# Ordering TensorE's pieces by width inside a visit, and charging changes of kind in the plan of a fused attention and MLP kernel

## The chip, the cores and the metric

The kernel runs on one core of one Trainium2 chip. The metric is the device time of one execution, in microseconds (us). The kernel before takes 345.28 us, the median of three runs (344.76 to 346.15).

## The reference, cut to what matters

Eight batches of eight heads attend over 576 tokens of width 64, with 16 extra "beacon" keys and values in front that every query may see; the token keys are causal. The result goes, token by token with its heads side by side, through an MLP of 512, 2048 and 512 columns with a sigmoid gate.

```python
k_all = np.concatenate([beacon_k, k], axis=2)           # 592 keys
v_all = np.concatenate([beacon_v, v], axis=2)
scores = 1/np.sqrt(D) * np.matmul(q, k_all.transpose(0, 1, 3, 2))
scores = np.where(causal, -1000000000.0, scores)        # beacons are never masked
a = np.exp(scores - scores.max(-1, keepdims=True))
a /= a.sum(-1, keepdims=True) + 1e-09
x = np.matmul(a, v_all).transpose(0, 2, 1, 3).reshape(B * S, H * D)   # 4608 x 512
h = x @ w_in                                            # 4608 x 2048
out = (h * (1.0 / (1.0 + np.exp(-1.702 * h)))) @ w_out  # 4608 x 512
```

## The kernel before, in words

**Sets.** Four heads of one batch make a *set*; there are 16 sets, two to a batch. For each set GpSimd's queue (POOL) loads q and k, with each head on 32 partitions and the two halves of the width as neighbouring elements. VectorE (DVE) transposes both (a *turn*, line 343). Beacon keys come by other queues, are cast (line 328) and transposed too (line 336). TensorE (PE) then makes scores with keys on the partitions and queries along the columns, four heads side by side in the array: a *quad* of four matmuls, one per head, 32 rows each, twice (`d` = 0 and 1, line 362). ScalarE (ACT) takes the exp into `E` (line 374). Masks set what is not causal to zero: on DVE for sets 0 and 1 (line 388), on POOL for all others (line 395). The maximum is not subtracted.

**Pieces and chunks.** A set has five key blocks of 128. Causality leaves, for queries 0 to 287, pieces of 288, 176 and 48 columns, and for queries 288 to 575 pieces of 288, 288, 288, 208 and 80: 1664 columns, one after the other in `E`. Scores are made in *chunks* of up to 512 columns into a PSUM tile `s` that exists once, so the next chunk waits for the exp of the one before. Sets 0 to 3 have four chunks each (512, 384, 384, 384). From set 4 on chunks of 512 run on from set to set, so one chunk may hold the end of one set and the start of the next, in pieces as they fall. There are 55 chunks, and `qk`*i* is chunk *i*.

**Sums and values.** `av`*s.x.half* (line 447) multiplies `E` of set *s* with values: *x* = 0 and 1 are the two halves of the width, *x* = 2 is a product with ones that gives the row sums; the output of one head is 32 columns wide. From set 4 on DVE first adds the key blocks of `E` together (`zadd`, line 426) into `zs`, so that *x* = 2 needs one or two quads instead of three to five: pieces of 112 (from `E`) and 176 (from `zs`) for the first half, 288 for the second. DVE turns sums into factors (`z1`: a transpose, line 458; `z2`: reciprocal, line 463, and a transpose, line 467) and multiplies them into `xT` while leaving PSUM (`norm`, line 476).

**MLP.** Groups of tokens, two of 256 and then eight of 512, go through `m1`*.g.n* (line 498, `xT` times `w_in`, 4 matmuls of 512 columns or 8 of 256), a tanh on ACT (line 512), a `gate` on DVE (line 519), and `m2`*.g.mt.qt* (line 531), a scale on ACT (line 545) and a store from SyncE's queue (SP, line 551).

**PSUM.** Beside `s` there is a ring of four buffers `u`. Every `m1`, every `av` and every `m2` row of 128 tokens takes one, and it is free again when its last reader is done: `gate`, `z1` or `norm`, or the scale of the output.

**What sets the order.** `Plan` is a list scheduler that runs while the program is built (lines 21 to 151). Each operation has an engine, an estimated duration, dependences, a priority `pr` (lower goes first) and a due time before which it isn't taken. The plan runs all engines in modelled time and the instructions are then emitted in that order, so each engine executes its own list in order. On PE, `choose` (line 129) prefers scores and values over the MLP, and stays with one *kind*: `r` for scores (32 rows), `c` for sums and values (32 columns), `m` for the MLP (the full array). A row of operations of one kind is a *visit*. A change of kind is charged 110 ns if the MLP is on one side and 90 otherwise:

```python
if o.mode != mode:
    dur += 110 if "m" in (mode, o.mode) else 90
```

On the other engines the ready operation of the lowest `pr` is taken (line 102). Chunks from the ninth on are due at equal steps from `T_ATT0` = 13000 to `T_ATT1` = 255000 ns of the plan's time (line 554), and loads, turns and casts have due times before that. Loads are all issued on POOL, at most eight in flight (line 565), between the masks of that engine.

Of the kernel before, what the change touches and what calls it, by code (L numbers as in the profile page):

```python
# [10 lines left out]
ALU = mybir.AluOpType  # L11


class Op:
    __slots__ = (
        "eng", "dur", "deps", "pr", "due", "emit", "kind", "ring", "mode", "lat",
        "start", "end", "left", "users", "ready", "seq", "name",
    )


class Plan:
# [8 lines left out]
        self.tiles = {}  # L30
        self.closers = {}

    def op(self, eng, dur, deps, emit, kind="", pr=5, due=0, ring=None, closes=None, mode=None, name=""):
        o = Op()
        o.eng, o.dur, o.emit, o.kind, o.pr, o.due = eng, dur, emit, kind, pr, due
        o.ring, o.mode, o.name = ring, mode, name
# [23 lines left out]
    def run(self):  # L60
# [3 lines left out]
        for o in self.ops:  # L64
            if o.left == 0:
                avail[o.eng].append(o)
        mode, last = "m", ""
        order = []
        todo = len(self.ops)
        while todo:  # L70
# [28 lines left out]
            if e == "PE":  # L99
                o = self.choose(ok, t, mode, last, free)  # L100
            else:
                o = min(ok, key=lambda o: (o.pr, o.ready, o.seq))
            dur = o.dur
            if e == "PE":
                if o.mode != mode:
                    dur += 110 if "m" in (mode, o.mode) else 90
                mode, last = o.mode, o.kind
                if o.ring is not None and o.ring not in self.tiles:
                    self.tiles[o.ring] = slot[1]
                    self.bank[slot[1]] = o.ring  # L110
# [44 lines left out]
def kernel(  # L155
# [11 lines left out]
    nc = tc.nc  # L167
# [90 lines left out]
    for s in range(EARLY, NSET):  # L258
# [75 lines left out]
    def e_turn(s, which):  # L334
# [10 lines left out]
            in_=f32(src[:, :]).rearrange("p (t c) -> p t c", t=TR),  # L345
        )

    def e_qk(i):
        sc = pss.tile([P, Q, 512], F32, tag="s", name="s")
        ss[i] = sc  # L350
        o = 0
        for (s, c0, c1) in CHUNKS[i]:
            if s not in Es:
                Es[s] = ep.tile([P, Q, ETOT], F16, tag="E", name="E")
            for (j, a, e), col in zip(PIECES, ecol):
                u, v = max(c0, col), min(c1, col + e - a)
                if u >= v:
                    continue
                for d in range(2):
                    for h in range(Q):  # L360
                        r = 32 * h
                        nc.tensor.matmul(  # L362
                            sc[:, h, o : o + v - u],
                            kT[s % NB2][r : r + 32, j * P : (j + 1) * P, d],
                            qT[s % NB2][r : r + 32, a + u - col : a + v - col, d],
                            start=(d == 0),
                            stop=(d == 1),
                        )
                o += v - u

    def e_exp(i, n):
        s, c0, c1 = CHUNKS[i][n]
# [55 lines left out]
    def e_av(s, x, half):  # L428
        b, hs = divmod(s, HS)
        u = ring_tile(("av", s, x, half))  # L430
        E = Es[s]
        q0 = half * HF
        terms = []
        if x == 2 and s >= ZSUM:
            if half == 0:
                terms.append((P, 0, Z0, E, 0, True, True))
                terms.append((P, Z0, HF, zsum[s], 0, True, True))
            else:
                terms.append((P, 0, HF, zsum[s], ZW, True, True))
        else:  # L440
            n = len(AVP[half])
            for i, (j, a, e) in enumerate(AVP[half]):
                terms.append((min(P, NK - j * P), a - q0, e - q0, E, where(j, a), i == 0, i == n - 1, j))
        for kw, a, e, src, col, first, last, *j in terms:
            for h in range(Q):
                lhs = ones[0:kw, :] if x == 2 else vb[b % NB2][0:kw, j[0], Q * hs + h, x::2]
                nc.tensor.matmul(  # L447
                    u[32 * h : 32 * h + 32, a:e],
                    lhs,
                    src[0:kw, h, col : col + e - a],  # L450
                    start=first,
                    stop=last,
                )
# [171 lines left out]
    def chunk(i):  # L625
# [8 lines left out]
        w = 0  # L634
        for s, c0, c1 in CHUNKS[i]:
            for (_, a, e), col in zip(PIECES, ecol):
                x = min(c1, col + e - a) - max(c0, col)
                w += max(45, 2 * x / 2.4 + 6) if x > 0 else 0
        qks[i] = op(
            "PE", w, deps, lambda: e_qk(i), kind="qk", pr=0,  # L640
            due=T_ATT0 + T_CH * (i - NCH0) if i >= NCH0 else 0, mode="r", name=f"qk{i}",
        )
        for n, (s, c0, c1) in enumerate(CHUNKS[i]):
            x = exps[(i, n)] = op(
# [17 lines left out]
    def values(s):  # L662
        b, hs = divmod(s, HS)
        whole = s >= ZSUM
        order = [(2, 0), (2, 1), (0, 0), (1, 0), (0, 1), (1, 1)] if whole else [
            (x, h) for h in range(2) for x in (2, 0, 1)
        ]
        sums, z2 = [], {}
# [17 lines left out]
        for n, (x, half) in enumerate(order):  # L686
# [10 lines left out]
            avs[(s, x, half)] = op(  # L697
                "PE", sum(y / 2.4 + 6 for y in w), deps,
                lambda x=x, half=half: e_av(s, x, half), kind="av",
                pr=(16 * s + (n if whole else 8 * half)) if s >= HS else half,  # L700
                ring=key, mode="c", name=f"av{s}.{x}.{half}",
            )
            if x == 2:
                z1 = op("DVE", 410, [avs[(s, x, half)]], lambda h=half: e_z1(s, h), pr=0, closes=key, name="z1")
# [129 lines left out]
```

## The time and the profile before

| | us |
|---|---|
| median of three runs | 345.28 |
| the profiled execution | 344.9 |
| its span, first to last instruction | 343.2 |
| TensorE busy | 324.3 |
| VectorE busy | 236.8 |
| ScalarE busy | 202.3 |
| GpSimd busy | 113.5 |
| matmuls, number | 3864 |
| TensorE clock granted | 0.998 |

The profiled execution is one run, and the profile's durations add up to its span; what lies around the span is the start and the end of the execution. In lines with a line number, "x" is the count of instructions, "out<-in" names what is written and read, and shapes are partitions x elements. PE's busy time is modelled at each matmul's end, so two matmuls that follow each other closely overlap in it; start to start is the measure of what they cost. DVE's and ACT's durations overlap the next one's by about 0.1 us too. An engine whose line says "idle before <-releaser" waited that long for the releaser named. "PEld" is the loading of weights into the array.

### The profile page before, as it was taken

Reading aid. Unit: us, or ns where it says so; the run is one execution under the profiler, and the core shown is the slowest. Engines: PE = TensorE matmul, PEld = TensorE weight load, DVE = VectorE, ACT = ScalarE, POOL = GpSimd, SP = SyncE. Lnnn points to the kernel's source line nnn. Section 1 sums busy time; section 2 is a strip of 40 time slices with the busy share of each in tenths; the row PEclk is TensorE's granted clock in tenths of the full one; section 3 lists DMA queues with packets and bytes.
Section 4 is the critical chain, followed back from the end, with each engine's and each line's share of the span. In section 5 each row is a group of like instructions: output and inputs, shape, how many; then the busy total and the mean of one; then the engine's idle time right before and its main releaser. Section 6 shows DMA issues by size and latency. Waiting matters only on the chain.

```text
span 343.2 us, 9086 instructions
## 1 busy us (share of the span) xinstructions
PE 324.3 (94%) x3864; PEld 166.6 (49%) x3864; DVE 236.8 (69%) x460; ACT 202.3 (59%) x245; POOL 113.5 (33%) x184
## 2 busy tenths in 40 slices
PE   0699899999899999999999999999999999999995
PEld 0476565545354545454554454445544454444442
DVE  3859778499958889889988788797854344453310
ACT  1585686786647774867776766765664224454421
POOL 8753593463415631812463227312110000000000
PEclk9999999999999999999999999999999999999999
DMA  7999999539042924970459509300000100000111
GB/s 128 165 204 209 190 198 124 107 46 122 3 103 64 155 39 107 66 139 3 72 61 145 99 33 128 77 33 32 32 32 32 61 32 31 33 31 31 55 59 71
DMA packets 54120, 28.76 MB, mean 84 GB/s; under 512 B 41280, under 2 KB 45376, under 8 KB 54080
## 3 DMA queue, kind: packets, MB, share of 16 engines
q0 software_dynamic: 47552, 18.49, 45.8%
q1 hardware_dynamic: 6464, 9.69, 7.9%
q8 instruction: 30, 0.49, 0.6%
q14 instruction: 10, 0.08, 0.1%
q10 hardware_dynamic: 64, 0.01, 0.0%
HBM read 37.22 MB, written 9.44 MB: 136 GB/s over the span
## 4 chain that ended last, share of the span: by engine, by line
PE 86%; DVE 5%; ACT 4%; DMA 2%; issue 1%; POOL 1%; SPq 1%; DVEq 0%; ACTq 0%
PE u L531 35%; PE u L498 34%; PE u L447 9%; PE s L362 8%; ACT E L374 3%; DMA bkf<-in_beacon_k_dram 2%; DVE g L519 1%; DVE qT L343 1%; DVE zs L426 1%; ACT sig L512 1%; DVE kT L343 1%; POOL E L395 1%; DVE zt L458 1%; SPq L322 1%; DVE rz L467 0%
## 5 line engine op out<-in xcount | busy, mean ns | idle before, releaser
L498 PE MATMUL u<-xT,w 128*128 128x512 f16 (+1 forms) x640 | 145.5, 360 | 1.6 <-DVE xT L476 0.9
L531 PE MATMUL u<-w,g 128*128 128x512 f16 x576 | 142.0, 379 | 0.4 <-DVE zt L458 0.4
L519 DVE SCALAR_TENSOR_TENSOR g<-sig,u 128x512 f16<-128x512 f16 x144 | 96.9, 681 | 59.9 <-ACT sig L512 59.4
L512 ACT ACTIVATE sig<-u 128x512 f16<-128x512 f32 x144 | 85.5, 598 | 82.8 <-PE u L498 77.9
L374 ACT ACTIVATE E<-s 128x2048 f16<-128x2048 f32 (+3 forms) x64 | 98.6, 1556 | 29.5 <-PE s L362 29.2
L498 PEld LDWEIGHTS <-w 128*128 128x128 f16 x640 | 60.7, 98 | 63.1 <-issue 3.1
L395 POOL TENSOR_SCALAR_AFFINE_SELECT E<-E 128x448 f16<-128x448 f16 (+2 forms) x84 | 48.8, 606 | 123.3 <-ACT E L374 116.6
L531 PEld LDWEIGHTS <-g 128*128 128x128 f16 x576 | 54.5, 98 | 65.1 <-issue 2.0
L362 PE MATMUL s<-qT,kT 32*128 32x288 f16 (+12 forms) x1352 | 35.8, 236 | 11.6 <-DVE qT L343 10.8
L362 PEld LDWEIGHTS <-kT 32*128 32x128 f16 x1352 | 24.4, 95 | 33.2 <-issue 21.4
L545 ACT ACTIVATE osb<-u 128x512 f32<-128x512 f32 x36 | 21.5, 597 | 23.7 <-PE u L531 23.7
L426 DVE TENSOR_TENSOR zs<-zs,E 128x192 f16<-128x192 f16 (+3 forms) x48 | 28.1, 585 | 5.5 <-ACT E L374 2.5
L476 DVE TENSOR_TENSOR xT<-u,rz 128x288 f16<-128x288 f32 x64 | 26.3, 448 | 7.9 <-PE u L447 7.3
L447 PE MATMUL u<-E,vb 128*32 128x288 f16 (+4 forms) x1024 | 29.2, 258 | 0.2 <-DVE g L519 0.2
L303 POOL DMA_DIRECT2D vb<-in_v_dram x32 | 27.2, 864 | 3.3 <-DMA qn<-in_q_dram 1.8
L447 PEld LDWEIGHTS <-vb 128*32 128x32 f16 (+1 forms) x1024 | 22.1, 98 | 5.4 <-issue 2.1
L343 DVE STREAM_TRANSPOSE kT<-kn 128x576 f32<-128x576 f32 x16 | 20.1, 1257 | 2.1 <-DMA kn<-in_k_dram 1.6
L426 DVE TENSOR_TENSOR zs<-E 128x704 f16<-128x704 f16 (+1 forms) x24 | 16.5, 688 | 5.4 <-POOL E L395 3.1
L343 DVE STREAM_TRANSPOSE qT<-qn 128x576 f32<-128x576 f32 x16 | 19.9, 1241 | 0.1
L467 DVE STREAM_TRANSPOSE rz<-rc 128x288 f32<-128x288 f32 x32 | 15.3, 478 | 1.1
L458 DVE STREAM_TRANSPOSE zt<-u 128x288 f32<-128x288 f32 x32 | 13.8, 458 | 2.3 <-PE u L447 2.1
L287 POOL DMA_DIRECT2D qn<-in_q_dram x16 | 9.0, 563 | 4.1 <-DMA vb<-in_beacon_v_dram 1.9
(27 smaller groups left out, 67.2 us busy)
## 6 DMA issues: line engine op xcount, KB each, us to landing
out_dram<-osb SPq DMA_DIRECT2D x36, 256.0 KB, 2.0
kn<-in_k_dram POOLq DMA_DIRECT2D x16, 288.0 KB, 6.5
qn<-in_q_dram POOLq DMA_DIRECT2D x16, 288.0 KB, 6.0
vb<-in_v_dram POOLq DMA_DIRECT2D x24, 128.0 KB, 5.1
w<-in_moe_w_in_dram POOLq DMA_DIRECT2D x8, 256.0 KB, 9.0
w<-in_moe_w_out_dram POOLq DMA_DIRECT2D x4, 512.0 KB, 13.7
vb<-in_v_dram POOLq DMA_DIRECT2D x8, 112.0 KB, 3.9
vb<-in_v_dram POOLq DMA_DIRECT2D x8, 80.0 KB, 5.1
```

The source lines that it names most:

```text
L303: nc.gpsimd.dma_start(out=t[0 : hi - lo, j, h0:h1, :], in_=v[b, h0:h1, lo:hi, :].rearrange("h n d -> n h d"),)
L343: nc.vector.transpose(out=f32(dst.rearrange("p n e -> p (n e)")).rearrange("p (r t) -> p t r", t=TR), in_=f32(src[:, :]).rearrange("p (t c ...
L362: nc.tensor.matmul(sc[:, h, o : o + v - u], kT[s % NB2][r : r + 32, j * P : (j + 1) * P, d], qT[s % NB2][r : r + 32, a + u - col : a + v - ...
L374: nc.scalar.activation(out=Es[s][:, :, c0:c1], in_=ss[i][:, :, o : o + c1 - c0], func=AFT.Exp, scale=0.125,)
L395: nc.gpsimd.affine_select(out=blk, in_=blk, compare_op=ALU.is_ge, fill=0.0, base=off + (Nb if j == 0 else 0), pattern=[[0, Q], [1, w]], ch ...
L426: nc.vector.tensor_tensor(out=t[:, :, o : o + w], in0=x, in1=y, op=ALU.add)
L447: nc.tensor.matmul(u[32 * h : 32 * h + 32, a:e], lhs, src[0:kw, h, col : col + e - a], start=first, stop=last,)
L476: nc.vector.tensor_tensor(out=xT[:, 2 * hs + x, t0 : t0 + HF], in0=rings[("av", s, x, half)][:, 0:HF], in1=zs[(s, half)][1][:, :], op=ALU. ...
L498: nc.tensor.matmul(u[:, o : o + w], w1t[:, kp, nt * P : (nt + 1) * P], xT[:, kp, t0:t1], start=(kp == 0), stop=(kp == NKT - 1),)
L512: nc.scalar.activation(out=sig[:, 0:w], in_=rings[("m1", g, n0)][:, 0:w], func=AFT.Tanh, scale=0.851)
L519: nc.vector.scalar_tensor_tensor(out=gts[g][:, n0:n1, 0:w], in0=sigs[(g, n0)][:, 0 : n * w].rearrange("p (n w) -> p n w", n=n), scalar=1.0 ...
L531: nc.tensor.matmul(o[:, :], gts[g][:, nt, mt * P : (mt + 1) * P], w2t[:, nt, :], start=(nt == 0), stop=(nt == NNT - 1),)
```

## The change

Seven edits, in two places of the kernel: what is issued, and how the plan orders it.

1. *Scores* (`qk_pieces`, new). The pieces of a chunk are sorted by falling width, over the sets in it; if the narrowest is over 64 columns wide, it is cut into one of 32 columns less and one of 32, which comes last.
2. *Sums from set 4 on.* The first half's product goes as 176 (from `zs`), 80 and 32 columns instead of 112 and 176, and the second half's is put ahead of the first's.
3. *Charge.* Each PE operation has a `tail`, the width of its last piece (0 for the MLP). A change of kind is charged 95 ns and 0.75 of the time that the last piece takes at 2.4 columns a ns.
4. *DVE's choice.* If the operation that would be taken has `pr` over 0, and one with `pr` 0 (`z1`, `z2`, masks, first turns) gets ready within 140 ns, that one is taken and DVE waits for it. `norm` of sets 0 and 1 gets `pr` 0.
5. *Chunks.* The first chunk of sets 0 and 1 counts as two parts (288 and 224 columns), so it has two exp instructions.
6. *Masks.* Of sets 0 and 1, DVE keeps the three masks of the first half; the three of the second half go to POOL.
7. *Due times.* Chunks are due from 11000 to 245000.

The program has 4104 matmuls instead of 3864, DVE 6 instructions less, ACT 2 and POOL 6 more; the orders of all engines but SP change.

```diff
+NEAR = 140
@@ Plan.run
             else:
                 o = min(ok, key=lambda o: (o.pr, o.ready, o.seq))
+                if e == "DVE" and o.pr > 0:
+                    near = [x for x in avail[e] if x.pr == 0 and max(x.ready, x.due) <= t + NEAR]
+                    if near:
+                        o = min(near, key=lambda o: (o.ready, o.seq))
+                        t = max(t, o.ready, o.due)
             dur = o.dur
             if e == "PE":
                 if o.mode != mode:
-                    dur += 110 if "m" in (mode, o.mode) else 90
-                mode, last = o.mode, o.kind
+                    dur += 95 + 0.75 * tail / 2.4
+                mode, last, tail = o.mode, o.kind, o.tail
@@ chunks
+    DVM = (0, 1, 2)
     EARLY, ZSUM = 2 * HS, 2 * HS
+    SPLIT = True
...
-        CHUNKS += [[(s, 0, EHALF)]] + [[(s, EHALF + cut * i, EHALF + cut * (i + 1))] for i in range(3)]
+        CHUNKS += [[(s, 0, HF), (s, HF, EHALF)] if SPLIT and s < HS else [(s, 0, EHALF)]] + [[(s, EHALF + cut * i, EHALF + cut * (i + 1))] for i in range(3)]
@@ scores
+    def qk_pieces(i):
+        got, o = [], 0
+        for (s, c0, c1) in CHUNKS[i]:
+            for (j, a, e), col in zip(PIECES, ecol):
+                u, v = max(c0, col), min(c1, col + e - a)
+                if u < v:
+                    got.append((v - u, s, j, a + u - col, o))
+                    o += v - u
+        got.sort(key=lambda x: -x[0])
+        w, s, j, a, o = got[-1]
+        if w > 64:
+            got[-1:] = [(w - 32, s, j, a, o), (32, s, j, a + w - 32, o + w - 32)]
+        return got
...
-            for (j, a, e), col in zip(PIECES, ecol):
...
+        for (w, s, j, a, o) in qk_pieces(i):
+            for d in range(2):
+                for h in range(Q):
...
@@ e_av
             if half == 0:
-                terms.append((P, 0, Z0, E, 0, True, True))
                 terms.append((P, Z0, HF, zsum[s], 0, True, True))
+                terms.append((P, 32, Z0, E, 32, True, True))
+                terms.append((P, 0, 32, E, 0, True, True))
@@ due times, masks, values
-    T_ATT0, T_ATT1 = 13000, 255000
+    T_ATT0, T_ATT1 = 11000, 245000
...
-                    eng = "DVE" if s < HS else "POOL"
+                    eng = "DVE" if s < HS and m in DVM else "POOL"
...
-        order = [(2, 0), (2, 1), (0, 0), (1, 0), (0, 1), (1, 1)] if whole else [
+        order = [(2, 1), (2, 0), (0, 0), (1, 0), (0, 1), (1, 1)] if whole else [
...
-                w = [HF] if half else [Z0, ZW]
+                w = [HF] if half else [ZW, Z0 - 32, 32]
...
-                    pr=1, closes=key, name="norm",
+                    pr=1 if s >= HS else 0, closes=key, name="norm",
```

More of the change, by code (lines that the diff above doesn't have):

```diff
@@ L16 @@
         "eng", "dur", "deps", "pr", "due", "emit", "kind", "ring", "mode", "lat",
-        "start", "end", "left", "users", "ready", "seq", "name",
+        "start", "end", "left", "users", "ready", "seq", "name", "tail",
     )
@@ L31, in __init__, with op @@
         self.closers = {}
-    def op(self, eng, dur, deps, emit, kind="", pr=5, due=0, ring=None, closes=None, mode=None, name=""):
+    def op(self, eng, dur, deps, emit, kind="", pr=5, due=0, ring=None, closes=None, mode=None, name="", tail=0):
         o = Op()
         o.eng, o.dur, o.emit, o.kind, o.pr, o.due = eng, dur, emit, kind, pr, due
-        o.ring, o.mode, o.name = ring, mode, name
+        o.ring, o.mode, o.name, o.tail = ring, mode, name, tail
         o.deps = [d for d in deps if d is not None]
@@ L66, in run @@
                 avail[o.eng].append(o)
-        mode, last = "m", ""
+        mode, last, tail = "m", "", 0
         order = []
@@ L350, in e_qk @@
         ss[i] = sc
-        o = 0
         for (s, c0, c1) in CHUNKS[i]:
@@ L354, in e_qk @@
                 Es[s] = ep.tile([P, Q, ETOT], F16, tag="E", name="E")
-            for (j, a, e), col in zip(PIECES, ecol):
[L356 to L369, printed above, removed]
+        for (w, s, j, a, o) in qk_pieces(i):
+            for d in range(2):
+                for h in range(Q):
+                    r = 32 * h
+                    nc.tensor.matmul(
+                        sc[:, h, o : o + w],
+                        kT[s % NB2][r : r + 32, j * P : (j + 1) * P, d],
+                        qT[s % NB2][r : r + 32, a : a + w, d],
+                        start=(d == 0),
+                        stop=(d == 1),
+                    )
     def e_exp(i, n):
@@ L633, in chunk @@
             deps += [exps[(i - 1, n)] for n in range(len(CHUNKS[i - 1]))]
[L634 to L638, printed above, removed]
+        ps = [x[0] for x in qk_pieces(i)]
+        w = sum(max(45, 2 * x / 2.4 + 6) for x in ps)
         qks[i] = op(
             "PE", w, deps, lambda: e_qk(i), kind="qk", pr=0,
-            due=T_ATT0 + T_CH * (i - NCH0) if i >= NCH0 else 0, mode="r", name=f"qk{i}",
+            due=T_ATT0 + T_CH * (i - NCH0) if i >= NCH0 else 0, mode="r", name=f"qk{i}", tail=ps[-1],
         )
@@ L700, in values @@
                 pr=(16 * s + (n if whole else 8 * half)) if s >= HS else half,
-                ring=key, mode="c", name=f"av{s}.{x}.{half}",
+                ring=key, mode="c", name=f"av{s}.{x}.{half}", tail=w[-1],
             )
```

## The prediction, made before the changed kernel had run

> **What bounds the kernel now.** I read the page first, then the chain of waits, what TensorE (PE) waited for, busy time by stretch, and the timeline at the changes of kind. From the page, the first engine line and the chain by engine:
>
> ```profile
> PE 324.3 (94%) x3864; PEld 166.6 (49%) x3864; DVE 236.8 (69%) x460; ACT 202.3 (59%) x245; POOL 113.5 (33%) x184
> ...
> PE 86%; DVE 5%; ACT 4%; DMA 2%; issue 1%; POOL 1%; SPq 1%; DVEq 0%; ACTq 0%
> ```
>
> PE carries the time. So the question is what the change does to PE's own work, and to the moments in which PE stands still. By stretch (columns: busy us, and number of instructions in brackets):
>
> ```profile
> 8.70:21.00 12.30, 9.44 (x186) 6.54 (x186) 9.43 (x23) 7.52 (x6) 8.37 (x12) 1.00 1.58 177
> 21.00:60.00 39.00, 37.66 (x662) 25.50 (x660) 30.97 (x64) 27.66 (x30) 20.88 (x33) 1.00 1.33 184
> 60.00:92.00 32.00, 29.71 (x426) 14.91 (x425) 25.90 (x51) 22.49 (x28) 15.13 (x23) 1.00 0.58 75
> 92.00:343.20 251.20, 247.47 (x2594) 119.56 (x2592) 167.24 (x315) 143.31 (x183) 61.70 (x99) 1.00 0.36 63
> ```
>
> From 92 us to its last product PE hardly stops; between 60 and 92 us DVE is at 81% and PE loses 2.3 us of busy time. The waits of PE:
>
> ```profile
> PE s L362 <- DVE qT L343: 10.8, 2, 8.7
> PE u L447 <- DVE g L519: 1.6, 2, 1.4
> PE u L498 <- DVE xT L476: 0.9, 1, 0.9
> ```
>
> Busy time includes modelled ends, so I also took starts of matmuls from the trace: a gap beyond the usual spacing of that width is a stall. Stalls over 60 ns: 6.4 us before 20 us (2.34 for the second set's qT, the rest slow first matmuls and waits for exp), 1.8 from 20 to 40, 0.2 at 54.5, 3.2 from 60 to 92, and 0.5 after. The largest late one:
>
> ```profile
> 88.40 1.45 DVE L426 TENSOR_TENSOR zs<-zs,E 128x832 f16<-128x832 f16 x2 [0.54 <-POOL E L395]
> ...
> 89.78 0.68 DVE L519 SCALAR_TENSOR_TENSOR g<-sig,u 128x512 f16<-128x512 f16 x1
> ...
> 90.50 0.31 PE L447 MATMUL u<-zs,ones 128*32 128x288 f16 x4 [1.45 <-DVE g L519]
> ```
>
> A gate stood behind two partial sums on DVE, which had waited for a mask of POOL; that gate frees one of the four PSUM ring buffers, and PE stood 1.6 us for it. Ring buffers freed late by DVE are this kernel's stall. Last, the changes of kind:
>
> ```profile
> 38.45 0.52 PE L362 MATMUL s<-qT,kT 32*128 32x288 f16 x16
> 38.90 1.05 PE L498 MATMUL u<-xT,w 128*128 128x256 f16 x8
> ...
> 41.62 0.52 PE L362 MATMUL s<-qT,kT 32*128 32x192 f16 x16
> 42.07 0.41 PE L447 MATMUL u<-E,ones 128*32 128x288 f16 x12
> ...
> 47.43 0.64 PE L362 MATMUL s<-qT,kT 32*128 32x288 f16 x24
> 47.99 0.63 PE L447 MATMUL u<-E,vb 128*32 128x288 f16 x24
> ```
>
> These three visits of scores (column one is the start) end with pieces of 96, 192 and 48 columns; they stream 384, 384 and 512 columns twice. At 2.4 columns a ns that is 0.320, 0.320 and 0.427 us. Start to next start is 0.45, 0.45 and 0.56. The rest is 0.13 each time: it does not follow the last width. Over all undisturbed changes of kind, last start to next start is width/2.4 plus 84 to 98 ns, for widths from 32 to 512.
>
> **What the Trainium skill says.** "TensorEngine Tiling (Array Packing)", Key Properties: changing the tiling mode drains TensorE; the trace agrees, about 97 ns over the stream. "TensorE: Matmul & The Clock Gate", Single matmul latency: (398 + N)/2.4 ns warm, so a constant part and a part that is the stream itself; the trace agrees in form. The same page, under "Wait — 56ns, not 53.3ns?": starts never come closer than about 25 ns however small N is; here quads of 32 columns start 26 ns apart (median of 15), not 13.
>
> **The change part by part.** Order within a visit: the columns streamed are the same (212,992 of scores, 267,264 of values and sums in both programs), so sorting costs and brings nothing by itself. Narrow ends: 24 score visits get a split, which is 48 quads more (192 matmuls), and 12 sums one quad more (48): the 240 by which the program grows. Each adds the floor instead of its stream, 26 - 13.3, and 2.5 for the other piece, about 15 ns: 60 x 15 = +0.9 us, by summing each visit +0.85. The gain is the disputed part: last widths fall by 4736 columns over the score visits and by 2976 over values. If a drain grew by 0.75/2.4 ns a column, as the plan now charges, that were -2.4 us; the visits shown say zero, and the widest score ends (256) show at most 0.1 ns a column, -0.5. I take zero. Changes of kind: 147 become 143 in the instruction order, 4 x 97 ns = -0.39. Work of PE together: **+0.46 us**.
>
> First exp of sets 0 and 1 in two: 1877 ns becomes two of about 1.13 and 0.91 (1448 ns for 1536 and 1877 for 2048 elements give 0.84 ns an element and 0.16 fixed), +0.16 each. For set 0 it hides behind the second qT, which DVE ends at 11.8 us. That transpose also holds DVE, so no mask starts earlier. For set 1 the next scores wait for it: **+0.16**.
>
> Masks of the second halves of sets 0 and 1 from DVE to POOL: DVE sheds 310 + 422 + 310 ns a set, POOL takes 573 + 685 + 573. On POOL they stand among loads. By exp's ends at 19.7 and 22.3 us, the first delays the next k load from 19.4 to 20.3, the other two end at 23.4 and push the pair after by 1.0 and 0.4; later loads of v for batch 1 move under 1 us. These k and q are turned only after 31 us, v is used after 44: nothing. The values that need these masks start at about 24.4, a cover of 0.9 us.
>
> Near rule and priority of norms: the chain z1, reciprocal, transpose, norm takes 2.16 us for two norms without guests. In the new order the group of 256 tokens starts straight after the last values of set 1 (97 ns of PE work between, 2468 before), but no transposes stand inside its chain. Values end at 1.15 us after z1's start, the ring buffer comes at 1.87: stall 0.7, and 0.15 for the third values. Behind the norms DVE has a q and a k transpose (1.2 + 1.4), then the gate that frees the ring for the third product of that group: ready 4.3, freed 5.4, stall 1.1. Sum 1.97 where before has 0.33 + 0.95 + 0.11 = 1.4: **+0.6**. A score visit soon after has 1672 ns of PE work to cover an exp that needs 2.1: +0.4, for 0.22 of before at 54.5: **+0.2**.
>
> 60 to 92 us: the first whole set's sums move from 5.1 to 12.5 us of PE work behind its last scores, the next set's from 2.8 to 6.0 or more. The 1.6 us stall goes, for its partial sums are long ready. But gates still queue behind turns, partial sums and the two z chains: at the eighth first product of group 2 I find 0.65, then 0.25, 0.5 at the second sums, 0.2 and 0.75 at the values (gate of the last product only 1117 ns of work ahead). 2.4 for 3.2: **-0.8**.
>
> After 92 us: 0.54 before; one new tight place, a first product 235 ns behind sums whose z1 takes 0.6 (+0.4), and one sum 4.4 us behind its scores, where I put the need at 4.5; **+0.2**. Attention ends some 7 us of work earlier and the pure MLP end is that much longer, with DVE at 17 of 40 us: no change, PE does it either way. The SP queue keeps its order.
>
> Sum: 0.46 + 0.16 + 0.6 + 0.2 - 0.8 + 0.2 = +0.8. Span 343.2 becomes 344.0; the profiled execution took 344.9 with 1.7 around it, so 345.7; the median of the runs is 345.28, 0.4 over that execution, so **346.1 us**. What can be told from no change here is about 0.5%, 1.7 us.
>
> **Rivals.** *Stalls go and do not come back* (faster): the 3.2 us of 60 to 92 vanish, the group of 256 tokens costs what it did. 0.46 + 0.16 - 3.0 + 0.2 = -2.2, so 343.1. For it: the longer distances of sums. Against: the ring still has four buffers and DVE is at 81% there. *Narrow ends pay* (faster): 2.4 less than my sum, 343.7; the visits shown speak against. *Gates behind transposes* (slower): on DVE's queue a gate waits for a 1.25 us transpose or a partial sum that waits for POOL, and a full ring stops PE. It decides when a gate comes over 1.7 us after its product's end (0.6 tanh, 0.69 gate, latencies) with the ring's next user right behind; two more such places of 1.2 us in 28 to 92 us give +0.8 + 2.4, so 348.5. For it: that is what before shows at 88.8. Against: the plan knows DVE's load roughly. *Masks late on POOL*: if a load ahead of them waits 1.5 us longer, values stall 0.6; small, inside the range.
>
> **How the numbers follow.** The likeliest (346.1, own range 344.4 to 347.5) has 0.50; stalls gone 0.20; narrow ends 0.06; gates behind transposes 0.24. Faster by 0.5% (under 343.55): 0.16 of the second, 0.03 of the third, 0.03 of the first, 0.22. Slower (over 347.0): 0.22 of the last and 0.08 of the first, 0.30. Within: 0.48. The range 342.6 to 348.6 leaves about a tenth below (half of the stalls-gone case) and a tenth above (nearly half of the last).
>
> **What would show it.** Start to next start of score visits minus stream stays 0.13 to 0.15 with ends of 32; if it falls towards 0.06, narrow ends pay. PE has 4104 matmuls and under 1 us more stream. Around 39 us a first product waits for DVE's gate about 1 us. Between 60 and 92 us PE's stalls are 2 to 3 us, led by gates; none or over 5 makes me wrong. The stretch after 95 us has under 1 us of stalls; more there is a cause I have not seen.

## The result: no change, and the profile after

The changed kernel takes 345.23 us, the median of four runs (345.05 to 345.53). The kernel before took 345.02 beside it (four runs, 344.71 to 346.15). The ratio is 1.0001, with an interval of 0.9976 to 1.0026. A later set of 13 runs gave 345.23 again, beside 345.14 for the kernel before, ratio 0.9996 (0.9987 to 1.0006). Two executions far from all others, one of 1154.23 us of the kernel before and one of 560.15 us of the kernel without the near rule below, are slow runs and are left out of every median and ratio.

Line numbers shift: scores are L382 (L362 before), values and sums L467 (L447), first products L518 (L498), gates L539 (L519), turns L353 (L343), second products L551 (L531). From the page after, the engine line and the chain by engine:

```profile
PE 324.2 (94%) x4104; PEld 172.7 (50%) x4104; DVE 234.3 (68%) x454; ACT 203.6 (59%) x247; POOL 117.2 (34%) x190
...
PE 75%; DVE 11%; issue 5%; POOL 3%; ACT 3%; DMA 2%; SPq 1%; DVEq 0%; POOLq 0%; ACTq 0%
```

PE is as busy as before, with 240 matmuls more. The chain gives DVE 11% where it had 5%, though the end has not moved: a chain of near-equal branches is a weak witness for what bounds. Busy time by stretch (busy us of PE, PEld, DVE, ACT and POOL, instructions in brackets):

```profile
8.70:21.00 12.30, 9.31 (x211) 6.93 (x211) 8.61 (x23) 7.50 (x8) 8.77 (x13) 1.00 1.60 180
21.00:60.00 39.00, 37.41 (x712) 26.01 (x709) 29.82 (x59) 27.62 (x30) 22.75 (x37) 1.00 1.32 183
60.00:92.00 32.00, 31.09 (x469) 16.53 (x468) 26.68 (x54) 24.76 (x28) 17.14 (x29) 1.00 0.59 76
92.00:343.40 251.40, 246.39 (x2718) 123.09 (x2716) 165.93 (x314) 142.47 (x181) 61.03 (x95) 1.00 0.36 63
```

PE gained 1.4 us of busy time between 60 and 92 us (31.09 against 29.71) and lost 1.1 after 92 (246.39 of 251.4, against 247.47 of 251.2). The waits of PE (us in total, times, longest):

```profile
PE s L382 <- ACT E L393: 1.2, 3, 0.6
PE u L518 <- DVE g L539: 1.1, 2, 0.8
PE u L518 <- DVE xT L496: 0.7, 1, 0.7
PE u L518 <- DVE zt L478: 0.5, 1, 0.5
PE u L467 <- DVE g L539: 0.4, 2, 0.3
```

The 1.6 us that sums of values waited for a gate are gone. First products wait for a gate (0.5 before, 1.1 now) and for a `z1` instead.

By starts of matmuls, with stalls as in the prediction (a gap over 60 ns beyond the usual one of that width, 97 ns more at a change of kind), from PE's first start to its last:

| us | before | after |
|---|---|---|
| first start, last start | 8.71, 339.18 | 8.79, 339.38 |
| usual spacing of all pieces | 300.71 | 301.56 |
| changes of kind, 97 ns each | 147: 14.26 | 143: 13.87 |
| stalls before 20 us | 6.41 | 6.27 |
| stalls 20 to 40 | 1.82 | 2.07 |
| stalls 40 to 60 | 0.22 | 0 |
| stalls 60 to 92 | 3.2 | 1.5 |
| stalls after 92 | 0.54 | 2.4 |
| excesses under 60 ns | 3.31 | 2.89 |

The rows for spacing and for changes of kind are counts times a usual cost, not measured times: by them the pieces cost 0.85 more and the changes 0.39 less. The last row takes 0.42 of that back, so PE's own work came out the same within 0.1 us (318.28 before, 318.32 after); the first experiment shows why. The waits carry the rest: 60 to 92 us gave 1.7, and the stretch after 92 took 1.9 back. All entries together make +0.1 us.

### The profile page after: what moved, and what is told of

Read it like the earlier page. It is cut to its first block, busy times and chain, and to the rows that moved or that the text cites. A ratio compares the mean times of both kernels' runs of the same rounds, so it can differ in the third digit from the quotient of the medians.

```text
span 343.4 us, 9569 instructions
## 1 busy us (share of the span) xinstructions
PE 324.2 (94%) x4104; PEld 172.7 (50%) x4104; DVE 234.3 (68%) x454; ACT 203.6 (59%) x247; POOL 117.2 (34%) x190
## 4 chain that ended last, share of the span: by engine, by line
PE 75%; DVE 11%; issue 5%; POOL 3%; ACT 3%; DMA 2%; SPq 1%; DVEq 0%; POOLq 0%; ACTq 0%
PE u L551 33%; PE u L518 28%; PE u L467 7%; PE s L382 7%; ACT E L393 3%; DVE g L539 3%; DVE zs L445 2%; POOL E L414 2%; DMA bkf<-in_beacon_k_dram 2%; DVE qT L353 1%; DVE kT L353 1%; POOL vb L313 1%; DVE rz L487 1%; DVE zt L478 1%; DVE xT L496 1%
## 5 line engine op out<-in xcount | busy, mean ns | idle before, releaser
L518 PE MATMUL u<-xT,w 128*128 128x512 f16 (+1 forms) x640 | 145.7, 360 | 2.4 <-DVE g L539 1.1
L551 PE MATMUL u<-w,g 128*128 128x512 f16 x576 | 142.5, 379 | 0.0
L539 DVE SCALAR_TENSOR_TENSOR g<-sig,u 128x512 f16<-128x512 f16 x144 | 96.6, 681 | 64.0 <-ACT sig L532 63.2
L393 ACT ACTIVATE E<-s 128x2048 f16<-128x2048 f32 (+4 forms) x66 | 98.8, 1515 | 26.0 <-PE s L382 25.2
L414 POOL TENSOR_SCALAR_AFFINE_SELECT E<-E 128x512 f16<-128x512 f16 (+3 forms) x90 | 52.8, 612 | 118.3 <-ACT E L393 107.3
L518 PEld LDWEIGHTS <-w 128*128 128x128 f16 x640 | 60.7, 98 | 62.1 <-issue 2.9
L551 PEld LDWEIGHTS <-g 128*128 128x128 f16 x576 | 54.5, 98 | 63.4 <-issue 0.2
L382 PE MATMUL s<-qT,kT 32*128 32x32 f16 (+9 forms) x1544 | 36.0, 227 | 12.2 <-DVE qT L353 10.9
L382 PEld LDWEIGHTS <-kT 32*128 32x128 f16 x1544 | 28.5, 95 | 33.8 <-issue 21.4
L445 DVE TENSOR_TENSOR zs<-zs,E 128x192 f16<-128x192 f16 (+3 forms) x48 | 27.0, 563 | 4.6 <-ACT E L393 2.7
L467 PE MATMUL u<-E,vb 128*32 128x288 f16 (+4 forms) x1024 | 29.2, 258 | 0.8 <-DVE g L539 0.4
L467 PEld LDWEIGHTS <-vb 128*32 128x32 f16 (+1 forms) x1024 | 22.6, 98 | 4.6 <-issue 1.9
L353 DVE STREAM_TRANSPOSE kT<-kn 128x576 f32<-128x576 f32 x16 | 20.1, 1257 | 3.8 <-DMA kn<-in_k_dram 2.8
L353 DVE STREAM_TRANSPOSE qT<-qn 128x576 f32<-128x576 f32 x16 | 20.0, 1247 | 0.5 <-DMA qn<-in_q_dram 0.5
L297 POOL DMA_DIRECT2D kn<-in_k_dram x16 | 9.1, 569 | 2.8 <-DVE g L539 2.0
```

Source lines behind the costliest of these rows:

```text
L353: nc.vector.transpose(out=f32(dst.rearrange("p n e -> p (n e)")).rearrange("p (r t) -> p t r", t=TR), in_=f32(src[:, :]).rearrange("p (t c ...
L382: nc.tensor.matmul(sc[:, h, o : o + w], kT[s % NB2][r : r + 32, j * P : (j + 1) * P, d], qT[s % NB2][r : r + 32, a : a + w, d], start=(d = ...
L393: nc.scalar.activation(out=Es[s][:, :, c0:c1], in_=ss[i][:, :, o : o + c1 - c0], func=AFT.Exp, scale=0.125,)
L414: nc.gpsimd.affine_select(out=blk, in_=blk, compare_op=ALU.is_ge, fill=0.0, base=off + (Nb if j == 0 else 0), pattern=[[0, Q], [1, w]], ch ...
L445: nc.vector.tensor_tensor(out=t[:, :, o : o + w], in0=x, in1=y, op=ALU.add)
L467: nc.tensor.matmul(u[32 * h : 32 * h + 32, a:e], lhs, src[0:kw, h, col : col + e - a], start=first, stop=last,)
```

## The experiments

Each kernel ran beside the kernel before on the same chip, in five rounds, in three groups that have 344.97, 345.14 and 344.89 for the kernel before. Across groups I compare each kernel's distance from the kernel before beside it. The ratio is formed from the single runs and not from the two medians, so it can differ from theirs by up to 0.1%. "First to last start" is PE's.

| kernel | median us | before beside it | ratio to before (interval) | first to last start |
|---|---|---|---|---|
| changed kernel again | 345.23 | 345.14 | 0.9996 (0.9987 to 1.0006) | 330.98 |
| pieces as before | 344.18 | 344.97 | 0.9980 (0.9972 to 0.9987) | 330.18 |
| widest piece last | 344.51 | 344.97 | 0.9988 (0.9980 to 0.9995) | 330.17 |
| one turn later | 344.51 | 344.97 | 0.9984 (0.9978 to 0.9991) | 330.35 |
| masks all on DVE | 344.90 | 344.89 | 0.9998 (0.9990 to 1.0007) | 330.84 |
| old due times | 347.83 | 345.14 | 1.0083 (1.0066 to 1.0100) | 332.99 |
| old charge | 346.13 | 345.14 | 1.0036 (1.0019 to 1.0053) | 331.88 |
| no near rule | 348.94 | 345.14 | 1.0119 (1.0098 to 1.0140) | 334.62 |
| measured charge | 347.98 | 344.89 | 1.0088 (1.0072 to 1.0105) | 333.56 |
| two edits | 344.01 | 344.89 | 0.9970 (0.9962 to 0.9977) | 330.44 |
| two edits, PE warm | 343.98 | 344.89 | 0.9965 (0.9951 to 0.9978) | PE starts earlier |

One thing varies from profile to profile: a first product at about 26 us waits 0.3 to 0.7 us for a load of `w_in` in six of these profiles (0.71 in the changed kernel again), and not in the two that the section above compares. The medians average over that, the single profiles do not. Of the seven edits, the order of the two sums (part of edit 2) was undone in none of the kernels.

### Pieces as before, and the widest piece last

Is a narrow end worth anything? The plan and the order of the operations stay those of the changed kernel; only what each visit issues is changed. `sent` gives a chunk's pieces uncut, in the first kernel as they fall and in the second by rising width; the sums of the first half go as 112 and 176 columns again.

```diff
     def e_qk(i):
-        for (w, s, j, a, o) in qk_pieces(i):
+        for (w, s, j, a, o) in sent(i):
...
             if half == 0:
+                terms.append((P, 0, Z0, E, 0, True, True))
                 terms.append((P, Z0, HF, zsum[s], 0, True, True))
-                terms.append((P, 32, Z0, E, 32, True, True))
-                terms.append((P, 0, 32, E, 0, True, True))
```

> The changed kernel's instruction order on every engine, with the pieces of the kernel before: scores unsorted and uncut, first-half sums as 112 and 176. The columns at the ends of the visits are 6464 more in sum than in the changed kernel, and 240 matmuls are gone. Mine (a drain does not depend on the last width): TensorE streams 0.85 us less, same stalls, 344.4. Rival (a drain grows by 0.75/2.4 ns a column): 2.0 longer drains and 0.85 less stream, 346.4. In the trace, the gap from last start to next start minus width/2.4 stays at 84 to 98 ns (mine) or grows with the width (rival).

> As old_pieces, but the pieces of each chunk of scores by rising width, so that the widest comes last: last widths sum to 13456 columns more than in the changed kernel. Mine: as old_pieces within 0.5 us, 344.4. Rival: 4.2 longer drains and 0.85 less stream, 348.6.

They stand 0.79 and 0.46 us under the kernel before, and both intervals lie below 1; the changed kernel stands 0.09 over it. With the pieces as before, the usual spacing of all pieces falls back to 300.71 (from 301.56), and the stalls stay (12.5 us). The same two visits in the timeline of PE, first of the changed kernel, whose pieces are 192, 160, 32 and then 208, 96, 48, 32 columns:

```profile
43.85 0.54 PE L382 MATMUL s<-qT,kT 32*128 32x192 f16 x24
44.32 0.41 PE L467 MATMUL u<-E,ones 128*32 128x288 f16 x12
...
46.50 0.54 PE L382 MATMUL s<-qT,kT 32*128 32x208 f16 x32
46.97 0.63 PE L467 MATMUL u<-E,vb 128*32 128x288 f16 x24
```

and of the kernel with the widest piece last, where they are 192, 192 and then 80, 96, 208:

```profile
43.45 0.53 PE L393 MATMUL s<-qT,kT 32*128 32x192 f16 x16
43.90 0.40 PE L477 MATMUL u<-E,ones 128*32 128x288 f16 x12
...
46.08 0.53 PE L393 MATMUL s<-qT,kT 32*128 32x80 f16 x24
46.53 0.63 PE L477 MATMUL u<-E,vb 128*32 128x288 f16 x24
```

Start to next start is 0.47 us with an end of 32 columns and 0.45 with ends of 192 and 208. Over all such changes to sums and values, the last piece's start to the next kind's start is 100 ns for 32 columns (changed kernel) and 162, 178, 198 and 212 for 176, 208, 256 and 288 (widest last). From 32 to 288 columns that is 112 ns for 256 columns, 0.4375 ns a column. The stream itself is 0.4167, so the drain grows by 0.02 ns a column, where the changed plan charges 0.31. A drain that grows by the plan's price would have made the two kernels slower, 346.4 and 348.6 us; they are faster.

What a narrow end does bring is small, but not nothing. The count of 0.85 us takes 26 ns for every quad of 32 columns, also for one that ends a visit: with the 97 of the change, 123 ns. From the first start of such a quad to the next kind it is 113 (median of 22 changes from scores to sums and values). So the floor of 26 ns isn't paid at the end of a visit. Over the 41 undisturbed changes of the changed kernel that follow a piece of 32 columns this is about 0.4 us. It shows in the excesses under 60 ns: past 22 us those at changes of kind sum to -0.09 us there, to 0.34 with the pieces as before and to 0.49 with the widest last. From the product behind the stall at 38.7 us to the last start PE takes 299.67 us in the changed kernel, 299.34 with the pieces as before and 299.27 with the widest last. There the cuts cost 0.3 to 0.4 us net, not 0.85. The medians lie further apart (0.88 and 0.55 us), but the ratios differ by 0.16% and 0.08%, 0.55 and 0.28 us, and the intervals meet or overlap, so they can't tell 0.4 from 0.85.

### One turn later

Is the stall at 38.7 us a gate behind a transpose? The timeline of the changed kernel (column one is the start, in brackets the idle time before and what ended it):

```profile
36.57 1.25 DVE L353 STREAM_TRANSPOSE qT<-qn 128x576 f32<-128x576 f32 x1
37.45 0.60 ACT L532 ACTIVATE sig<-u 128x512 f16<-128x512 f32 x1 [5.65 <-PE u L518]
...
37.88 1.25 DVE L353 STREAM_TRANSPOSE kT<-kn 128x576 f32<-128x576 f32 x1
...
38.98 1.27 DVE L539 SCALAR_TENSOR_TENSOR g<-sig,u 128x512 f16<-128x512 f16 x2
39.71 1.03 PE L518 MATMUL u<-xT,w 128*128 128x256 f16 x8 [0.85 <-DVE g L539]
```

The tanh ends at 38.05, and the gate starts at 38.98, behind the turn of set 3's k. The edit moves that one operation behind the gates of the first two products:

```diff
     order = plan.run()
+    order.remove(turn[(3, 1)])
+    order.insert(order.index(gates[(1, 2)]) + 1, turn[(3, 1)])
```

> The changed kernel with one move on VectorE's queue: the k transposes of set 3 after the gate of the second first-product of the second group of 256 tokens, in place of before the gate of the first. Mine: the stall of 0.92 us at 38.7 us was TensorE waiting for a PSUM buffer whose gate stood behind that transpose; it falls under 0.2, and nothing later gives it back: 344.4, span 0.8 shorter. Rival: the scores or the next gate behind take the wait over, 345.2.

Its timeline:

```profile
37.77 0.69 DVE L539 SCALAR_TENSOR_TENSOR g<-sig,u 128x512 f16<-128x512 f16 x1 [0.26 <-ACT sig L532]
...
38.51 1.03 PE L518 MATMUL u<-xT,w 128*128 128x256 f16 x8
38.64 0.69 DVE L539 SCALAR_TENSOR_TENSOR g<-sig,u 128x512 f16<-128x512 f16 x1 [0.18 <-ACT sig L532]
...
39.48 1.26 DVE L353 STREAM_TRANSPOSE kT<-kn 128x576 f32<-128x576 f32 x1
39.57 1.02 PE L551 MATMUL u<-w,g 128*128 128x512 f16 x4
```

The 0.92 us stall is gone, which shows the cause. But two second-layer products now come before their loads of `w_out` and wait, 0.20 at 39.3 and 0.22 at 41.8, so something later did give part of it back. By starts of matmuls 0.5 of 0.92 is kept, and the median agrees: 0.46 us under the kernel before, where the changed kernel is 0.09 over. In its profile PE also started 0.56 earlier (8.24 against 8.79), which is no part of the edit.

### Masks all on DVE

Does it matter that three masks a set went to POOL, and that the first exp was split? The six masks of sets 0 and 1 go back to DVE, the exp to one instruction; PE's order is the same.

```diff
-    DVM = (0, 1, 2)
+    DVM = (0, 1, 2, 3, 4, 5)
...
-    SPLIT = True
+    SPLIT = False
```

> The changed kernel with all masks of sets 0 and 1 on VectorE and the first exp of these sets in one piece, as before; TensorE's order is the same as in the changed kernel. Mine: the move of the masks costs and brings nothing and the second exp instruction costs 0.16, so 345.1, within 0.5 of the changed kernel. Rival (the masks on GpSimd are late for the values of sets 0 and 1, or hold back loads): 0.5 to 1.5 faster than the changed kernel. Other rival (VectorE needed the relief): gates and norms before 40 us come later and it is 0.5 to 2 slower.

344.90 against 344.89 before, and from 30 us on the stalls are those of the changed kernel, place by place. These two edits together are worth nothing that these runs can tell (interval 0.9990 to 1.0007).

### The plan's three edits, one undone at a time

```diff
-    T_ATT0, T_ATT1 = 11000, 245000
+    T_ATT0, T_ATT1 = 13000, 255000
```

> The changed kernel with the due times of before (13000 to 255000). Counted from its order: TensorE's work 0.2 us more than in the changed kernel (145 changes of kind); the sums of the second whole set 4.4 us of work behind its scores instead of 6.0. Mine: the stalls past 92 us come from where ring buffers meet VectorE's queue, not from the pace, so they stay between 1 and 3 us, and 4.4 costs at most 0.2: 345.5. Rival (attention set closer is what brought the stalls past 92 us): they fall to 0.5 as in before, 343.9. Second rival (the due times alone took the stall of 1.6 us away): it comes back near 88 us, 346.9.

```diff
-                    dur += 95 + 0.75 * tail / 2.4
+                    dur += 110 if "m" in (mode, o.mode) else 90
```

> The changed kernel with the charge of before for a change of kind (110 and 90 ns) in the plan; the pieces stay sorted and cut. Counted from its order: 147 changes of kind, TensorE's work 0.4 us more; sums of the whole sets 5.1 us behind their scores. Mine: the charge only reshuffles; 0.4 more work and stalls within 1 us of the changed kernel's: 345.6, between 344.6 and 346.6. Rival (the charge is what spares the stall of 1.6 us at 88): it comes back, 347.2.

```diff
-                if e == "DVE" and o.pr > 0:
+                if False and e == "DVE" and o.pr > 0:
...
-                    pr=1 if s >= HS else 0, closes=key, name="norm",
+                    pr=1, closes=key, name="norm",
```

> The changed kernel without the rule that VectorE waits up to 140 ns for an operation of priority 0, and with norms of sets 0 and 1 at priority 1. Counted from its order: 151 changes of kind, TensorE's work 0.8 us more; sums of the first three whole sets 4.2, 4.3 and 4.8 us behind their scores, where about 4.5 are needed. Mine: 0.8 more work and 0.2 to 0.6 more in waits for sums: 346.4. Rival (the rule does nothing for TensorE): work alone, 346.0; if waiting on VectorE cost time, faster than the changed kernel.

All three are slower than both the kernel before and the changed one: by 2.6, 0.9 and 3.7 us against the changed kernel on the same chip. None of the three brought the kernel before back: each gives another order again (145, 147 and 151 changes of kind) with stalls in other places. The third takes back the near rule and the priority of the norms at once.

*Old due times.* It took 347.8, more than I (345.5) and either rival had said. I had looked for the stalls past 92 us to shrink or to stay; they rose to about 4.5 us, and between 77 and 84 us another 1.2 appeared. Part of its timeline:

```profile
77.42 1.25 DVE L353 STREAM_TRANSPOSE qT<-qn 128x576 f32<-128x576 f32 x1
77.63 0.24 PE L467 MATMUL u<-E,ones 128*32 128x80 f16 x8
77.80 1.04 PE L551 MATMUL u<-w,g 128*128 128x512 f16 x4
78.52 0.79 DVE L478 STREAM_TRANSPOSE zt<-u 128x288 f32<-128x288 f32 x2
79.01 1.89 PE L518 MATMUL u<-xT,w 128*128 128x512 f16 x8 [0.17 <-DVE zt L478]
...
81.16 1.02 PE L518 MATMUL u<-xT,w 128*128 128x512 f16 x4 [0.27 <-DVE g L539]
```

Sums end, the `z1` that frees their buffers stands behind a turn, and then three gates stand behind the z chain (`z1` and `z2` of both halves). The changed kernel has the second half of this at 167 us (below): there no turn stands ahead of `z1`.

*Old charge.* Within what I expected in size, but not in place: the 1.6 us stall of the kernel before did not come back at 88 us. The profile has one of 2.0 us at 53.6 instead, inside values, for which its list of waits names no releaser ("issue"):

```profile
PE u L467 <- issue: 1.8, 1, 1.8
```

The place in the timeline:

```profile
53.57 0.30 PE L467 MATMUL u<-E,vb 128*32 128x288 f16 x2
```

Two matmuls of a quad start at 53.57 and the other two at 55.71. All four read the same `E` and the same loads of values, so a missing operand is unlikely, but what held PE there isn't shown, and how often it happens isn't known from one profile. It is more than the 0.9 us by which this kernel is slower than the changed one.

*No near rule.* I had expected about 346.4; it took 348.9. Its waits of PE, and two stretches by the clock granted (the third number from the end):

```profile
PE s L382 <- ACT E L393: 2.7, 4, 1.4
PE s L382 <- DVE E L407: 2.0, 1, 2.0
PE u L467 <- DVE g L539: 1.9, 2, 1.4
```

```profile
34.00:38.40 4.40, 2.26 (x88) 1.76 (x80) 4.32 (x8) 1.88 (x1) 2.82 (x5) 1.00 1.20 207
38.40:43.00 4.60, 4.16 (x71) 2.69 (x71) 2.46 (x7) 3.15 (x3) 2.18 (x5) 0.63 1.79 180
```

In 34 to 38.4 us PE is busy 2.26 of 4.4 us, with stalls of 0.83 and 1.47, and 0.52 just after: PE waits for a turn of q, for an exp and for a norm, and the norms stand behind two turns (at 36.03 and 37.74), so no product is ready in between. Then TensorE's clock falls, to 0.50 from 39.4 to 42.8 us (0.63 is the mean of the whole stretch): products of 256 columns start 213 ns apart instead of 109. So a row of stalls cost more than its own length. "TensorE: Matmul & The Clock Gate", Part 1, of the Trainium skill says that the clock is gated to half after a window of about 3.4 us without activity; here it fell although PE was busy for 1.57 of the 3.4 us ahead of it (36.0 to 39.4), so here a stretch that was partly busy was enough. Gates later stall another 1.6 at 93.4 us, and the order has 151 changes of kind for 143 (0.78 us).

### The measured charge

If the width is worth nothing, a flat charge is the truer one.

```diff
-                    dur += 95 + 0.75 * tail / 2.4
+                    dur += 97
```

> The changed kernel with a change of kind charged at 97 ns whatever the last width, which is what the trace shows. Counted from its order: 149 changes of kind, TensorE's work 0.6 us more, sums of whole sets 4.4 us or more behind their scores. Mine: a charge that is nearer the truth gives no better order, 345.8, between 344.8 and 347. Rival (the truth pays): under 344.5.

347.98 us, 0.9% slower than before and above the 344.8 to 347 that I expected. It has 149 changes of kind, and 3.4 us of stalls between 80 and 100 us, with the same look: a turn and two gates ahead of a z chain.

```profile
89.13 1.25 DVE L353 STREAM_TRANSPOSE kT<-kn 128x576 f32<-128x576 f32 x1
...
90.23 1.27 DVE L539 SCALAR_TENSOR_TENSOR g<-sig,u 128x512 f16<-128x512 f16 x2
90.96 0.31 PE L467 MATMUL u<-zs,ones 128*32 128x288 f16 x4 [0.74 <-DVE g L539]
...
94.25 0.53 PE L467 MATMUL u<-E,vb 128*32 128x288 f16 x9 [1.25 <-DVE g L539]
```

Here a truer price in the plan gave a worse order. With three charges there are three orders, whose counted work differs by 0.6 us at most and whose times, each against the kernel before beside it, by 3.0: the charge picks one order out of many, and the stalls of that order decide. Three orders don't show that a truer price is worse in general.

### Two edits together, and PE kept warm

The two edits that helped touch different engines: pieces as before, and the later turn.

> The changed kernel's order with the pieces of before and the k transposes of set 3 moved behind two gates. Mine: 0.85 less stream, and of the 0.9 us stall about 0.5 is kept, since the second layer's weights land right behind it: 343.9, ratio 0.996 to 0.998. Rival (the two are swallowed by the same later wait): 344.5.

344.01 us: 0.3% under the kernel before. The interval lies below 1, so it is a gain, though one smaller than the 0.5% that I set as the bound for the prediction. Over the pieces alone (0.9980) it is 0.1% more, and the two intervals overlap, so the medians don't show that the two gains add up. In the profile the stall at 38.7 us is gone, but the start is longer: PE waited 3.63 us for the second set's qT, against 2.29 with the pieces alone.

The last kernel adds 20 products of zeros, ahead of everything, to use the 8.7 us in which PE waits for its first data:

```diff
+    idle = cst.tile([P, 512], F16, tag="idle", name="idle")
+    nc.vector.memset(idle, 0.0)
+    first = psu.tile([P, 512], F32, tag="u0", name="u0")
+    for i in range(20):
+        nc.tensor.matmul(first[:, :], idle[:, 0:P], idle[:, :], start=True, stop=True)
```

> As both, with 20 products of a zeroed tile (128x128 by 512) on TensorE between 1.5 and 8.5 us, before its first scores. The first products run at half rate up to 21 us, some 3 us over their later rate. Mine: exp, masks and the landing of the first layer's weights near 26.5 us and of the second's near 39.5 stand behind, so at most 1 us is kept: 343.2. Rival (TensorE's rate alone sets this stretch): 2.5 us, 341.4.

It took 343.98, the same as the two edits alone, where I had expected 343.2 and the rival 341.4. Its timeline of PE and two stretches:

```profile
8.39 0.64 PE L397 MATMUL s<-qT,kT 32*128 32x288 f16 x24 [0.85 <-DVE qT L358]
11.47 1.04 PE L397 MATMUL s<-qT,kT 32*128 32x288 f16 x24 [2.44 <-DVE qT L358]
```

```profile
8.30:9.10 0.80, 0.64 (x24) 0.51 (x23) 0.47 (x4) 0.00 (x1) 0.80 (x2) 1.00 1.14 182
11.40:18.00 6.60, 5.74 (x130) 4.09 (x131) 5.40 (x18) 3.59 (x4) 4.66 (x8) 0.50 1.53 179
```

The first visit of scores ran at the full rate (0.64 us, 1.04 in the changed kernel). Then PE idled 2.44 us for the second set's qT, and the same visit took 1.04 again: the clock was back at 0.50 until about 18 us. Between the last of the added products (7.54) and 11.47 us PE had worked 0.64 of 3.93 us. "TensorE: Matmul & The Clock Gate", Part 1, gives an idle window of about 3.4 us; the idle time here is 3.29 in all, in two parts, so again the work in between did not hold the clock up. Warming PE ahead of its first data is lost in the wait for the second.

## Why the prediction was right, and where it was wrong

I predicted 346.1 us, range 342.6 to 348.6, no change that can be told as the likeliest case. Measured: 345.23. The span was to be 344.0 and was 343.4, and the 0.4 from the profiled execution to the median of three runs did not repeat (the changed kernel's profiled execution took 345.13, its median is 345.23). The time came out nearer than the steps, by luck, as the last paragraph says. By its own terms:

- *A drain that grows with the last width, taken as zero: right.* 0.02 ns a column against the plan's 0.31. Of the rivals, "narrow ends pay" is refuted by the two kernels on pieces.
- *Work of PE, +0.46: too large.* The counts are as predicted, +0.85 for the cut pieces and -0.39 for four changes of kind less, but the work came out at +0.04. The prediction charged the floor of 26 ns to both quads of every cut piece. The one that ends a visit doesn't pay it; the prediction's own reading, width/2.4 plus 84 to 98 ns at a change, had left no room for it. Undoing the cuts saved 0.3 to 0.4 us past 39 us, not 0.85.
- *Exp in two, +0.16: not seen.* The visit behind it waited 0.64 us for an exp (0.58 before), but stalls before 20 us fell by 0.14 in all, and undoing the split and the masks changed nothing that can be measured.
- *Masks on POOL, zero: right,* as far as a run that also took the second exp back can tell.
- *Group of 256 tokens, 1.97 us of stalls: right.* Measured 0.27 + 0.74 + 0.92 = 1.93, the last behind the turn that the prediction named, as the later turn showed. The stretch rose by 0.25 rather than 0.6, since before had 0.42 of small stalls between 20 and 21 us, at the slow rate of the start, that were not in my comparison (0.14 after).
- *Wait for an exp, +0.2: right.* 0.48 at 65.45 us for 0.4 predicted.
- *60 to 92 us, 2.4 left of 3.2: right in kind, too large.* The places are there but smaller: 0.29 for 0.65 at the eighth first product, 0.31 for 0.5 at the second sums, 0.43 for 0.95 at values, nothing for 0.25. Together 1.0 us; I had let DVE's queue run later than it did. With the wait for an exp the stretch has 1.5 us, under the 2 to 3 that I gave as the sign, and that wait, not a gate, is the longest.
- *After 92 us, 0.7: the step that failed.* Measured 2.4, where the prediction said that over 1 us would be a cause it had not seen. The place that I had named is in the timeline of the changed kernel:

```profile
167.21 0.23 PE L467 MATMUL u<-E,ones 128*32 128x80 f16 x8
167.36 0.85 DVE L478 STREAM_TRANSPOSE zt<-u 128x288 f32<-128x288 f32 x2 [0.41 <-PE u L467]
167.89 1.89 PE L518 MATMUL u<-xT,w 128*128 128x512 f16 x8 [0.46 <-DVE zt L478]
...
169.34 1.85 DVE L539 SCALAR_TENSOR_TENSOR g<-sig,u 128x512 f16<-128x512 f16 x3
170.05 1.02 PE L518 MATMUL u<-xT,w 128*128 128x512 f16 x4 [0.27 <-DVE g L539]
```

The product behind the sums waits 0.53 for `z1`, for 0.4 predicted. What I left out is what comes next: three gates queue behind that z chain, so the third product of the row waits 0.43 for the first of them. And I had no entry for 127 to 129 us, where values wait for a norm and for gates behind a turn that starts at 126.06 (0.30 + 0.37 + 0.11):

```profile
126.06 1.25 DVE L353 STREAM_TRANSPOSE qT<-qn 128x576 f32<-128x576 f32 x1
...
127.16 0.44 DVE L496 TENSOR_TENSOR xT<-u,rz 128x288 f16<-128x288 f32 x1
...
127.53 1.26 DVE L539 SCALAR_TENSOR_TENSOR g<-sig,u 128x512 f16<-128x512 f16 x2
127.66 0.41 PE L467 MATMUL u<-E,vb 128*32 128x288 f16 x12 [0.23 <-DVE xT L496]
```

The five other stalls there make 0.68, about the 0.54 of before. I followed DVE's queue closely up to 92 us and took what came later from the kernel before. No run here took the stalls after 92 us away by themselves, so their cause is read from the timeline, not shown by an experiment.

The errors of the two last steps, 1.3 us too much and 1.7 too little, cancelled, and the work of PE was 0.4 too much, so the predicted time came out better than the steps, by luck. The case "stalls gone" came half true for 60 to 92 us (1.7 of 3.2 went) and wrong for the whole. "Gates behind transposes" named the kind of wait that, by the timeline, undid the gain, but looked for it between 28 and 92 us and for 1.2 us a place; it came after 92, at 0.3 to 0.5 a place, and at 167 us the gates stand behind a z chain and no turn. In the orders with old due times and with the measured charge it was larger: stalls of 4.5 us after 92 us, and of 3.4 between 80 and 100.

## What to carry to other kernels

A change of kind on TensorE costs a constant beyond the stream of its last piece (here some 97 ns), so ending a visit on a narrow piece hardly shortens the drain (0.02 ns a column). It spares that piece its floor, 10 ns here, and cutting a piece to get there costs more than that. In a kernel whose order comes out of a list scheduler, every price, due time or priority reshuffles where the buffers' last readers stand in their engine's queue: compute the direct cost of an edit, but then walk that queue to the end of the program, behind each release as well as up to it. Here the six orders that differ in the plan took 345 to 349 us with counted work within 1.3 us. A gain in one stretch is only a gain when the later ones have been looked at, and a truer model is no promise of a better order.

## What the runs showed of the hardware

- A row of short stalls can cost the clock: with PE busy for 1.57 of 3.4 us, the next 3.4 us ran at a granted 0.50, with 256 columns in 213 ns instead of 109. An idle time of 2.44 us, after a 0.64 us visit and 0.85 us of idle time, was followed by the same at the start.
- A quad of 32 columns takes 26 ns from its start to the next of its kind, 13 more than its stream. Ahead of a change from scores to sums or values it doesn't take these 13: from its start to the next kind it is the stream and 100 ns, and the stream and 104 for 288 columns.
- The granted clock can't be read before its first recorded change: the changed kernel reads 1.00 from 8.7 us on, though its 256-column products start 213 ns apart until about 19.6 us; with PE warmed up ahead, the same stretch reads 0.50.
